# Starting the first chunk of an MLP's forward and backward pass on half its rows: eight PSUM groups on 256 rows, w1 by rows, the other rows by DMA transpose

## The chip, the cores and the metric

The kernel runs on one core of one Trainium2 chip. The metric is device time in microseconds of that core; lower is better. Besides the device time, each run lists the span of the core's own work.

## The reference

```python
def _fwd_reference(x, w1, w2):              # x: 1 x 2048 x 640, w1: 640 x 1536, w2: 1536 x 640, bf16
    h = jnp.einsum("bsd,df->bsf", x, w1)
    h = _silu(h)
    out = jnp.einsum("bsf,fd->bsd", h, w2)
    return out

def reference(x, w1, w2, grad_out):
    _out, _vjp = jax.vjp(_f, x, w1, w2)     # _f is _fwd_reference
    return (_out, *_vjp(grad_out))          # out, grad x, grad w1, grad w2
```

## The kernel before

The kernel works through 2048 rows in four chunks of 512 (`SC`). For each chunk it computes h transposed (12 groups of 128 columns of w1, each five matmuls deep, in one PSUM bank each), its SiLU and what the gradient needs, then `out` ("the second phase" below: `w2_nat` with `aT`), then the gradients. The first chunk has nothing to hide its loads behind. Its head is what the change touches:

```python
    LAG_G = 4; KM = 2; NWARM = 22
    # ... NWARM matmuls on a constant tile keep TensorE busy while x is loaded ...
    early += [load_x_half(0), load_x_half(1), load_w1_rows(0, 1), load_w1_rows(1, KM)]   # 2 x 320 KB of x, 2 x 128 KB of w1
    load_w1_rows(KM, DT)                       # columns 0:512 of the other three row blocks of w1
    for fc in range(1, NFC):
        load_w1(fc * FC, (fc + 1) * FC)        # w1 columns 512:1024, 1024:1536, 640 KB each
    nc.sync.dma_start(out=w2_nat[:], in_=w2_v[:])
    goT_next = load_goT(0)                     # DMA transpose
    # ... DMA transposes of w2 and w1 ...

    def pe_x_half(xT, half):                   # 10 TensorE transposes, 5 copies; called for both halves
        for dt_ in range(DT):
            tp = ps_h.tile([P, 2, P], dt_in, name="tp", tag="hp")
            for q in range(2):
                nc.tensor.transpose(tp[:, q, :], x_two[:, half, q, dt_ * P:(dt_ + 1) * P], ident[:])
            copy(out=xT[:, dt_, lo:lo + 2 * P].rearrange("p (s q) -> p q s", q=2), in_=tp[:])

    def h_first(xT, aT, ghT):
        # ... four banks ...
        for dt_ in range(KM):
            for ft in range(FB):               # FB = 4 groups
                h_mm(hps[ft], ft, xT, dt_, dt_ + 1)          # 512 rows of x at once
        for i in range(FT + LAG_G):            # FT = 12 groups
            if i < FT:
                # ... the rest of group i: 3 matmuls if i < FB, else 5 in a new bank ...
                silu_a(i, hps[i], aT)
            if i >= LAG_G:
                silu_grad(i - LAG_G, hps[i - LAG_G], aT, ghT)
```

## Time and profile before

| | before |
|---|---|
| device time, median of the first 3 runs | 320.69 us (320.67 to 320.93) |
| span of the profiled run | 319.4 us |
| first matmul of h | 5.30 us |
| TensorE clock reaches full rate | 6.22 us |
| second phase starts | 18.71 us |

From the page of the kernel before: the span, the busy time of each engine with its share of the span, the chain of waits by engine, and the group of all h matmuls (busy time, mean ns of one, idle time before them).

```profile
span 319.4 us, 3541 instructions
PE 314.6 (98%) x1469; PEld 146.3 (46%) x1498; DVE 102.6 (32%) x182; ACT 77.9 (24%) x142; POOL 0.7 (0%) x6
PE 98%; DMA 1%; issue 1%; DVE 0%; DVEq 0%; SPq 0%
L206 PE MATMUL hp<-xT,w_nat 128*128 128x512 bf16 x238 | 57.2, 381 | 0.1
```

TensorE is the bottleneck and almost never waits. The durations of single matmuls overlap (381 ns each, but one starts every 216 ns), so starts are what to count. Next, TensorE alone in the timeline of the first 20 us (start, duration of the stretch, engine, line, instruction, count).

```profile
0.50 2.53 PE L145 MATMUL wp<-warm 128*128 128x128 bf16 x22 [0.50 <-DVE warm L141]
3.19 2.31 PE L197 MATMUL tp<-ident,x_two 128*128 128x128 bf16 x20 [0.16 <-DMA x_two<-in_x_dram]
5.30 13.57 PE L206 MATMUL hp<-xT,w_nat 128*128 128x512 bf16 x58
18.71 1.46 PE L269 MATMUL hp<-aT,w_nat 128*128 128x512 bf16 x6
```

Here is the whole room for a better start: 22 warm-up matmuls until x arrives, 20 transposes, then h without a gap. (Two of the 60 h matmuls are missing from the records.) Last, the early transfers in the DMA view (count, KB each, median us from issue to landing). The two halves of x landed at 3.15 and 4.02 us, and w2 at 17.01 us.

```profile
w_nat<-in_w_dram SPq DMA_DIRECT2D x1, 1920.0 KB, 13.4
x_two<-in_x_dram SPq DMA_DIRECT2D x2, 320.0 KB, 3.3
w_nat<-in_w_dram SPq DMA_DIRECT2D x1, 384.0 KB, 4.5
w_nat<-in_w_dram SPq DMA_DIRECT2D x2, 128.0 KB, 3.7
```

### The profile page before, as it was taken

The page shows a single profiled execution, that of the slowest core. Times are in us where ns is not written, and L with a number is a line of the kernel's source. Part 1 is how long each engine was busy: PE and PEld are TensorE (multiplying, and loading weights), DVE is VectorE, ACT ScalarE, POOL GpSimd, SP SyncE. Part 2 cuts the span into 40 slices and gives each one's busy share as a digit, 9 for nine tenths or more (in the row PEclk, how much of TensorE's full clock was granted, in tenths as well). Part 3 has the DMA queues.
Part 4 walks back from the last instruction along what each step waited for, and adds up shares of the span by engine and source line. Part 5 has one row for each costly group of instructions (what it writes and reads, how often), then busy time and mean ns, then how long its engine had stood idle before and what let it go on. Part 6 is the DMA issues. An engine that isn't in the chain of part 4 may idle for free.

```text
span 319.4 us, 3541 instructions
## 1 busy us (share of the span) xinstructions
PE 314.6 (98%) x1469; PEld 146.3 (46%) x1498; DVE 102.6 (32%) x182; ACT 77.9 (24%) x142; POOL 0.7 (0%) x6
## 2 busy tenths in 40 slices
PE   9999999999999999999999999999999999999996
PEld 6444444444444444444444444444444444444443
DVE  3771541477410087710147741000000100001001
ACT  4960000545201254411054520110100001001100
POOL 0000000000000000000000000000000000000000
PEclk9999999999999999999999999999999999999999
DMA  8999999999999855292634079819999998995111
GB/s 282 307 180 222 246 292 264 341 263 292 293 278 271 223 190 140 86 308 76 171 114 133 2 259 267 217 30 294 265 212 257 267 240 292 253 294 182 49 37 45
DMA packets 147312, 67.33 MB, mean 211 GB/s; under 512 B 112609, under 2 KB 147041, under 8 KB 147297
## 3 DMA queue, kind: packets, MB, share of 16 engines
q1 hardware_dynamic: 147296, 67.12, 80.9%
q8 instruction: 11, 0.18, 0.2%
q14 instruction: 5, 0.03, 0.0%
HBM read 9.83 MB, written 28.97 MB: 121 GB/s over the span
## 4 chain that ended last, share of the span: by engine, by line
PE 98%; DMA 1%; issue 1%; DVE 0%; DVEq 0%; SPq 0%
PE hp L269 32%; PE hp L206 16%; PE hp L357 16%; PE hp L253 16%; PE hp L406 15%; PE hp L387 1%; DMA x_two<-in_x_dram 1%; PE tp L197 1%; DVE g L398 0%; DVEq L398 0%; SPq L434 0%
## 5 line engine op out<-in xcount | busy, mean ns | idle before, releaser
L206 PE MATMUL hp<-xT,w_nat 128*128 128x512 bf16 x238 | 57.2, 381 | 0.1
L253 PE MATMUL hp<-goT,w2T 128*128 128x512 bf16 x232 | 56.4, 379 | 0.4
L269 PE MATMUL hp<-aT,w_nat 128*128 128x512 bf16 x235 | 52.2, 379 | 0.3
L269 PE MATMUL hp<-ghT,w1T 128*128 128x512 bf16 x235 | 52.2, 379 | 0.3
L357 PE MATMUL hp<-a_blk,go_nat 128*128 128x512 bf16 x236 | 51.8, 379 | 0.2
L406 PE MATMUL hp<-gh_blk,x_nat 128*128 128x512 bf16 x219 | 48.2, 379 | 0.3
L277 ACT ACTIVATE oT<-hp 128x512 bf16<-128x512 f32 x24 | 14.3, 598 | 109.8 <-PE hp L269 109.8
L215 ACT ACTIVATE aT<-hp 128x512 bf16<-128x512 f32 x48 | 29.9, 625 | 33.0 <-PE hp L206 33.0
L206 PEld LDWEIGHTS <-w_nat 128*128 128x128 bf16 x240 | 23.6, 99 | 28.4 <-issue 0.6
L269 PEld LDWEIGHTS <-w1T 128*128 128x128 bf16 x240 | 23.5, 98 | 28.3
L357 PEld LDWEIGHTS <-go_nat 128*128 128x128 bf16 x240 | 23.5, 98 | 28.3
L253 PEld LDWEIGHTS <-w2T 128*128 128x128 bf16 x240 | 23.5, 98 | 28.3
L269 PEld LDWEIGHTS <-w_nat 128*128 128x128 bf16 x240 | 23.5, 98 | 28.4
L279 DVE CAST oT<-hp 128x512 bf16<-128x512 f32 x16 | 11.1, 692 | 77.0 <-PE hp L269 63.5
L260 DVE SCALAR_TENSOR_TENSOR ghT<-ghT,hp 128x512 bf16<-128x512 bf16 x48 | 32.5, 682 | 7.3 <-PE hp L253 7.3
L406 PEld LDWEIGHTS <-x_nat 128*128 128x128 bf16 x224 | 21.9, 98 | 26.4
L222 DVE SCALAR_TENSOR_TENSOR ghT<-aT,v 128x512 bf16<-128x512 bf16 x48 | 32.8, 687 | 0.5
L221 DVE TENSOR_SCALAR v<-t 128x512 bf16<-128x512 f32 x48 | 20.3, 426 | 30.5 <-ACT t L219 30.5
L219 ACT ACTIVATE t<-hp 128x512 f32<-128x512 f32 x48 | 29.8, 625 | 0.0
L417 DVE CAST g<-hp 128x512 bf16<-128x512 f32 x7 | 4.8, 692 | 47.0 <-PE hp L406 27.4
L367 DVE CAST g2T<-hp 128x512 bf16<-128x512 f32 x7 | 4.8, 692 | 46.1 <-PE hp L357 46.1
L365 ACT ACTIVATE g2T<-hp 128x512 bf16<-128x512 f32 x8 | 4.8, 597 | 47.0 <-PE hp L357 40.8
(20 smaller groups left out, 27.0 us busy)
## 6 DMA issues: line engine op xcount, KB each, us to landing
aT_scr<-aT SPq DMA_DIRECT2D x4, 1536.0 KB, 6.2
ghT_scr<-ghT SPq DMA_DIRECT2D x4, 1536.0 KB, 8.0
out_dram<-o_sb SPq DMA_DIRECT2D x8, 640.0 KB, 3.6
oT_scr<-oT SPq DMA_DIRECT2D x4, 640.0 KB, 3.6
go_nat<-in_grad_out_dram SPq DMA_DIRECT2D x4, 640.0 KB, 6.4
x_nat<-in_x_dram SPq DMA_DIRECT2D x4, 640.0 KB, 5.3
gxT_scr<-oT SPq DMA_DIRECT2D x4, 640.0 KB, 4.7
w_nat<-in_w_dram SPq DMA_DIRECT2D x1, 1920.0 KB, 13.4
```

The costliest lines, as they stand in the source:

```text
L206: nc.tensor.matmul(hp[:], lhsT=w1_nat[:, dt_, ft * P:(ft + 1) * P], rhs=xT[:, dt_, :], start=(dt_ == 0), stop=(dt_ == DT - 1),)
L215: nc.scalar.activation(aT[:, ft, :], hp[:], ACT.Silu)
L219: nc.scalar.activation(t[:], hp[:], ACT.Tanh, scale=0.5)
L221: nc.vector.tensor_scalar(out=v[:], in0=t[:], scalar1=-0.5, scalar2=0.5, op0=ALU.mult, op1=ALU.add)
L222: nc.vector.scalar_tensor_tensor(out=ghT[:, ft, :], in0=aT[:, ft, :], scalar=1.0, in1=v[:], op0=ALU.subtract, op1=ALU.mult)
L253: nc.tensor.matmul(gp[:], lhsT=w2T[:, dt_, ft * P:(ft + 1) * P], rhs=goT[:, dt_, :], start=(dt_ == 0), stop=(dt_ == DT - 1),)
L260: nc.vector.scalar_tensor_tensor(out=ghT[:, ft, :], in0=ghT[:, ft, :], scalar=1.0, in1=gp[:], op0=ALU.add, op1=ALU.mult)
L269: nc.tensor.matmul(op_[:], lhsT=w_all[:, ft, dt_ * P:(dt_ + 1) * P], rhs=rhs_all[:, ft, :], start=(ft == 0), stop=(ft == FT - 1),)
L277: nc.scalar.activation(oT[:, dt_, :], op_[:], ACT.Copy)
L279: nc.vector.tensor_copy(out=oT[:, dt_, :], in_=op_[:])
L357: nc.tensor.matmul(gp[:], lhsT=go_nat[:, st, dt_ * P:(dt_ + 1) * P], rhs=a_blk[:, st, :], start=(st == 0), stop=(st == ST - 1),)
L406: nc.tensor.matmul(gp[:], lhsT=x_nat[:, st, dt_ * P:(dt_ + 1) * P], rhs=gh_blk[:, st, :], start=(st == 0), stop=(st == ST - 1),)
```

## The change

Its intent is to begin h after 256 rows of x instead of 512. Eight groups fill all eight PSUM banks of the program (`ps_h` has eight buffers) on those rows, going through w1 row block by row block, so w1 is loaded in pieces of 1024 columns (2 KB rows). The other 256 rows come by a DMA transpose, which saves ten of the twenty transposes on TensorE. VectorE copies the first four banks to SBUF, so that groups 8 to 11 find banks without waiting for the gradient's tanh.

```diff
-    LAG_G = 4
-    KM = 2
-    NWARM = 22
+    NWARM = 21
+    HC = 2 * P
+    NG = 8
+    NCOPY = FT - NG
+    GC = NG * P
 ...
-        early += [load_x_half(0), load_x_half(1), load_w1_rows(0, 1), load_w1_rows(1, KM)]
-        load_w1_rows(KM, DT)
+        early += [load_x(nc.sync, 0), load_x(nc.scalar, 1)]
+        early += [load_w1(k, k + 1, slice(0, GC)) for k in range(3)]
+        load_w1(3, DT, slice(0, GC))
+        nc.sync.dma_start_transpose(out=xT_next[:, :, HC:SC], in_=x2[HC:SC, :])
+        load_w1(0, DT, slice(GC, F))
 ...
+        def pe_x(xT):                        # 10 transposes into three banks, three copies
+            slices = ((0, 1), (1, 3), (3, DT))
 ...
+            for dt_ in range(DT):
+                for ft in range(NG):
+                    h_mm(hs[ft], ft, xT, dt_, dt_ + 1, slice(0, HC))
+            for ft in range(NG):
+                h_mm(hs[ft], ft, xT, 0, DT, slice(HC, SC))
+                silu_a(ft, hs[ft], aT)
+                if ft < NCOPY:
+                    h_sb = hpool.tile([P, SC], FP32, name="h_sb")
+                    nc.vector.tensor_copy(out=h_sb[:], in_=hs[ft][:])
+                    hs[ft] = h_sb
+            for ft in range(NG, FT):
+                hs.append(ps_h.tile([P, SC], FP32, name="hp"))
+                h_mm(hs[ft], ft, xT, 0, DT)
+                silu_a(ft, hs[ft], aT)
+                silu_grad(ft - NG + NCOPY, hs[ft - NG + NCOPY], aT, ghT)
 ... (the other silu_grad follow)
```

More of the change, by code (lines that the diff above doesn't have):

```diff
@@ L137 @@
         tpool = mctx.enter_context(tc.tile_pool(name="tpool", bufs=3))
+        hpool = mctx.enter_context(tc.tile_pool(name="hpool", bufs=NCOPY))
         opool = mctx.enter_context(tc.tile_pool(name="opool", bufs=2))
@@ L165, with load_x, load_w1 @@
         xT_next = xpool.tile([P, DT, SC], dt_in, name="xT")
-        x_two = cpool.tile([P, 2, 2, D], dt_in, name="x_two")
-        def load_w1(lo, hi):
-            nc.sync.dma_start(out=w1_nat[:, :, lo:hi], in_=w1_v[:, :, lo:hi])
-        def load_x_half(half):
-            lo = half * 2 * P
-            return nc.sync.dma_start(
-                out=x_two[:, half, :, :], in_=x2[lo:lo + 2 * P, :].rearrange("(p q) d -> p q d", q=2)
-            )
-        def load_w1_rows(lo, hi):
-            return nc.sync.dma_start(out=w1_nat[:, lo:hi, 0:FC], in_=w1_v[:, lo:hi, 0:FC])
-        early += [load_x_half(0), load_x_half(1), load_w1_rows(0, 1), load_w1_rows(1, KM)]
-        load_w1_rows(KM, DT)
+        def load_x(eng, q):
+            return eng.dma_start(out=x_nat[:, q, :], in_=x_v[:, q, :])
+        def load_w1(lo, hi, cols):
+            return nc.sync.dma_start(out=w1_nat[:, lo:hi, cols], in_=w1_v[:, lo:hi, cols])
+        early += [load_x(nc.sync, 0), load_x(nc.scalar, 1)]
[3 more added lines that the diff above has]
+        load_w1(0, DT, slice(GC, F))
         start_before_entry_wait(nc, {i.ins.name for i in early})
-        for fc in range(1, NFC):
-            load_w1(fc * FC, (fc + 1) * FC)
         nc.scalar.activation(warm_a[:], warm[:, 0:1], ACT.Silu)
@@ L190, with h_mm @@
         nc.sync.dma_start_transpose(out=w1T[:], in_=w1[:, :])
-        def pe_x_half(xT, half):
-            lo = half * 2 * P
-            for dt_ in range(DT):
-                tp = ps_h.tile([P, 2, P], dt_in, name="tp", tag="hp")
-                for q in range(2):
-                    nc.tensor.transpose(tp[:, q, :], x_two[:, half, q, dt_ * P:(dt_ + 1) * P], ident[:])
-                copy = nc.scalar.copy if dt_ % 2 else nc.vector.tensor_copy
-                copy(out=xT[:, dt_, lo:lo + 2 * P].rearrange("p (s q) -> p q s", q=2), in_=tp[:])
-        pe_x_half(xT_next, 0)
-        pe_x_half(xT_next, 1)
-        def h_mm(hp, ft, xT, lo, hi):
+        def pe_x(xT):
+            slices = ((0, 1), (1, 3), (3, DT))
+            tps = [ps_h.tile([P, hi - lo, 2, P], dt_in, name="tp", tag="hp") for lo, hi in slices]
+            for q in range(2):
+                for tp, (lo, hi) in zip(tps, slices):
+                    for dt_ in range(lo, hi):
+                        nc.tensor.transpose(
+                            tp[:, dt_ - lo, q, :], x_nat[:, q, dt_ * P:(dt_ + 1) * P], ident[:]
+                        )
+            for k, (tp, (lo, hi)) in enumerate(zip(tps, slices)):
+                copy_tp = nc.scalar.copy if k % 2 else nc.vector.tensor_copy
+                copy_tp(out=xT[:, lo:hi, 0:HC], in_=tp[:].rearrange("p k q s -> p k (q s)"))
+        def h_mm(hp, ft, xT, lo, hi, cols=slice(0, SC)):
             for dt_ in range(lo, hi):
                 nc.tensor.matmul(
-                    hp[:],
+                    hp[:, cols],
                     lhsT=w1_nat[:, dt_, ft * P:(ft + 1) * P],
-                    rhs=xT[:, dt_, :],
+                    rhs=xT[:, dt_, cols],
                     start=(dt_ == 0),
@@ L232, in h_first @@
         def h_first(xT, aT, ghT):
-            hps = []
-            for ft in range(FB):
-                hps.append(ps_h.tile([P, SC], FP32, name="hp"))
-            for dt_ in range(KM):
-                for ft in range(FB):
-                    h_mm(hps[ft], ft, xT, dt_, dt_ + 1)
-            for i in range(FT + LAG_G):
-                if i < FT:
-                    if i < FB:
-                        h_mm(hps[i], i, xT, KM, DT)
-                    else:
-                        hps.append(ps_h.tile([P, SC], FP32, name="hp"))
-                        h_mm(hps[i], i, xT, 0, DT)
-                    silu_a(i, hps[i], aT)
-                if i >= LAG_G:
-                    silu_grad(i - LAG_G, hps[i - LAG_G], aT, ghT)
+            pe_x(xT)
+            hs = [ps_h.tile([P, SC], FP32, name="hp") for ft in range(NG)]
+            for dt_ in range(DT):
[13 more added lines that the diff above has]
+                silu_grad(ft - NG + NCOPY, hs[ft - NG + NCOPY], aT, ghT)
+            for ft in list(range(NCOPY)) + list(range(NG, FT)):
+                silu_grad(ft, hs[ft], aT, ghT)
         def g_group(ft, goT, ghT):
@@ L296 @@
                 for j in range(0, ST, STC):
-                    nc.sync.dma_start(out=x_nat[:, j:j + STC, :], in_=x_v[:, j:j + STC, :])
+                    rows = slice(max(j, 2), j + STC)
+                    nc.sync.dma_start(out=x_nat[:, rows, :], in_=x_v[:, rows, :])
             if c == 0:
```

## The prediction

> **What bounds the kernel.** TensorE: 98% busy of a 319.4 us span (the page), and the chain of waits is TensorE from 3.19 us to the tail. In the trace the 512-column matmuls start every 216 ns from 6.4 to 313 us without a wait. 1440 x 0.2158 = 310.8 us is fixed, and the change doesn't touch it. Only the head (first h matmul at 5.30 us) and a cold stretch (the first two h matmuls took 419 and 427 ns, full rate from about 6.2 us) can move: at most some 2 us, under 1%.
>
> **Removed.** Ten of twenty PE transposes, 107 ns apart at the cold rate: 1.07 us. The first copies wait for 320 KB of x instead of 640 KB; the two halves landed at 3.15 and 4.0 us, so x is complete near 3.1 us. Transposes run about 2.9 to 3.9 us; the copy of the first slice (0.45 us, 0.35 us after its transposes) ends near 4.2 us. First h matmul: about 4.25 us, 1.05 us earlier.
>
> **Added.** Forty more matmuls (80 of 256 columns for 40 of 512), about 2.5 ns each: 0.1 us. Weight loads stay hidden: in the last block 384-column matmuls start every 162 ns and 128-column ones every 56 ns. Four VectorE copies of about 0.69 us; VectorE (32% busy) has slack. More cold time: [...]107 ns per 128 columns before 6.2 us, 56 ns in the last block. I expect the doubling near 6.2 us again; starting 1.05 us earlier in the cold gains only half of that.
>
> **Moved.** w1 comes in 256 KB pieces. From the landings of before (320 KB at 3.15, 640 at 4.0, 1280 at 6.5 us) I estimate them at 3.9, 4.8 and 5.6 us and the 512 KB at 7.2 us. h on 256 rows needs them at 4.25, 6.0, 6.9 and 7.8 us: no wait. The DMA transpose of rows 256 to 511 follows in the queue; 640 KB transposes took 3.1 to 3.7 us of queue in the trace, so 1.6 to 1.9 us for half: landing near 9.0 us. The first eight groups reach it near 9.5 us: just no wait. w2 (landed 17.0, needed 18.7 us) comes about 0.8 us later, at 17.8; needed at 18.2: tight. goT, w2T, w1T have 7 us of slack. The first banks are free by 13 us, group 8 needs one near 13.9 us; ScalarE started activations every 0.48 us here and keeps up.
>
> **Sum.** -1.05 (earlier start) + 0.53 (cold half) + 0.1 (overhead) = -0.4 us; tight arrivals may take some back. Predicted time **320.3 us**, range 319.5 to 321.1. Chances: faster by over 2%: 0.005; within 2%: 0.985; slower by over 2%: 0.01.
>
> **What would show it.** In the timeline: first h matmul at 4.0 to 4.5 us; 213 ns per 256-column matmul until about 6.2 us, 109 ns after; the second 256 columns begin at 9.3 to 9.9 us without a TensorE gap over 0.3 us; the second phase (w2_nat with aT) starts near 18.2 us instead of 18.7; later stages unchanged. Idle TensorE before the second 256 columns would show the transpose late; idle before the second phase, w2 late.
>
> **What would make it wrong.** The transpose or w2 over 0.5 us later: no gain, or up to 1 us slower. The clock doubling earlier than 6.2 us (gain up to 1 us), or later through the gap between transposes and h. x late through the ScalarE queue. Nothing here reaches 2% (6.4 us).

(The sum: -1.05 + 0.53 + 0.1 = -0.42 us. The 0.53 us in it is an estimate from the measured 107 and 56 ns per 128 columns and from the 6.2 us of one trace.)

## The result, and the profile after

| | before | after |
|---|---|---|
| device time, median | 320.80 us (4 runs, 320.67 to 320.93) | 320.71 us (4 runs, 320.49 to 321.03) |
| span of the profiled run | 319.4 us | 319.3 us |
| first matmul of h | 5.30 us | 3.94 us |
| TensorE clock reaches full rate | 6.22 us | 3.49 us |
| second phase starts | 18.71 us | 18.57 us |

The ratio is 0.9998, with a 95% interval of 0.9981 to 1.0015. (A ratio is the mean time of one kernel's fast runs over that of the other's fast runs of the same rounds, so it isn't quite the ratio of the medians quoted here.) The two kernels can't be told apart in this test. From the page of the kernel after:

```profile
span 319.3 us, 3597 instructions
PE 313.3 (98%) x1499; PEld 148.6 (47%) x1527; DVE 103.0 (32%) x182; ACT 77.2 (24%) x139; POOL 0.7 (0%) x6
PE 96%; DMA 2%; issue 1%; DVE 0%; DVEq 0%
L204 PE MATMUL hp<-xT,w_nat 128*128 128x512 bf16 (+1 forms) x272 | 56.9, 348 | 1.8 <-DMA w_nat<-in_w_dram 1.2
```

The h matmuls now stand idle 1.8 us, mostly for w1, and the chain of waits has gained a DMA. TensorE in the timeline after:

```profile
0.50 2.42 PE L148 MATMUL wp<-warm 128*128 128x128 bf16 x21 [0.50 <-DVE warm L144]
2.71 1.10 PE L195 MATMUL tp<-ident,x_nat 128*128 128x128 bf16 x10
3.94 1.91 PE L204 MATMUL hp<-xT,w_nat 128*128 128x256 bf16 x16
6.85 1.05 PE L204 MATMUL hp<-xT,w_nat 128*128 128x256 bf16 x8 [1.00 <-DMA w_nat<-in_w_dram]
8.13 10.60 PE L204 MATMUL hp<-xT,w_nat 128*128 128x256 bf16 x75 [0.23 <-DMA w_nat<-in_w_dram]
18.57 1.67 PE L270 MATMUL hp<-aT,w_nat 128*128 128x512 bf16 x7
```

h starts 1.36 us earlier, and it runs at full rate from its first matmul (109 ns from start to start). Then it stops twice: 16 matmuls, a gap, 8 matmuls, a second gap. From start to start these gaps are 1.27 and 0.505 us where 0.109 is normal, so TensorE lost 1.16 + 0.40 = 1.56 us. The DMA view and the chain of waits (start, duration, what) name the cause. First the DMA view:

```profile
w_nat<-in_w_dram SPq DMA_DIRECT2D x1, 1920.0 KB, 13.3
w_nat<-in_w_dram SPq DMA_DIRECT2D x3, 256.0 KB, 3.8
w_nat<-in_w_dram SPq DMA_DIRECT2D x1, 512.0 KB, 6.0
x_nat<-in_x_dram SPq DMA_DIRECT2D x1, 160.0 KB, 2.6
x_nat<-in_x_dram ACTq DMA_DIRECT2D x1, 160.0 KB, 2.9
```

Then the chain of the first 20 us:

```profile
2.04 6.05 DMA w_nat<-in_w_dram
8.09 0.04 issue
8.13 6.50 PE hp L204 x57
```

The 512 KB of w1 that were issued at 2.04 us landed at 8.09 us, and everything after is TensorE without a gap. What follows that landing is fixed: 16 + 40 matmuls of 109 ns and 20 of 216 ns are 10.42 us, and 8.13 + 10.42 = 18.55 us is the start of the second phase. So in this trace the landing of the last early w1 piece sets the time, and nothing that happened before it matters.

The rest of the program did not change. The span minus the start of the second phase is 300.72 us before and 300.68 us after; over all fourteen profiles it is 300.67 to 300.72 us. The start of the second phase therefore stands for the whole kernel below.

### The profile page after: what moved, and what is told of

It reads as the page before. It is cut to its first block, busy times and chain, and to the rows that moved or that the text cites. A ratio compares the mean times of both kernels' runs of the same rounds, so it can differ in the third digit from the quotient of the medians.

```text
span 319.3 us, 3597 instructions
## 1 busy us (share of the span) xinstructions
PE 313.3 (98%) x1499; PEld 148.6 (47%) x1527; DVE 103.0 (32%) x182; ACT 77.2 (24%) x139; POOL 0.7 (0%) x6
## 4 chain that ended last, share of the span: by engine, by line
PE 96%; DMA 2%; issue 1%; DVE 0%; DVEq 0%
PE hp L270 32%; PE hp L254 16%; PE hp L359 16%; PE hp L204 15%; PE hp L408 15%; DMA w_nat<-in_w_dram 2%; PE hp L389 1%; DVE g L400 0%; DVEq L400 0%
## 5 line engine op out<-in xcount | busy, mean ns | idle before, releaser
L204 PE MATMUL hp<-xT,w_nat 128*128 128x512 bf16 (+1 forms) x272 | 56.9, 348 | 1.8 <-DMA w_nat<-in_w_dram 1.2
L204 PEld LDWEIGHTS <-w_nat 128*128 128x128 bf16 x280 | 27.1, 98 | 26.4 <-DMA w_nat<-in_w_dram 2.1
L213 ACT ACTIVATE aT<-hp 128x512 bf16<-128x512 f32 x48 | 28.6, 606 | 36.7 <-PE hp L204 36.7
L270 PEld LDWEIGHTS <-w_nat 128*128 128x128 bf16 x240 | 23.4, 98 | 28.4
L217 ACT ACTIVATE t<-hp 128x512 f32<-128x512 f32 x44 | 26.1, 598 | 0.5 <-DVE v L219 0.5
```

The lines of the kernel that those rows point to most:

```text
L204: nc.tensor.matmul(hp[:, cols], lhsT=w1_nat[:, dt_, ft * P:(ft + 1) * P], rhs=xT[:, dt_, cols], start=(dt_ == 0), stop=(dt_ == DT - 1),)
L213: nc.scalar.activation(aT[:, ft, :], hp[:], ACT.Silu)
L217: nc.scalar.activation(t[:], hp[:], ACT.Tanh, scale=0.5)
L270: nc.tensor.matmul(op_[:], lhsT=w_all[:, ft, dt_ * P:(dt_ + 1) * P], rhs=rhs_all[:, ft, :], start=(ft == 0), stop=(ft == FT - 1),)
```

## The experiments

All twelve runs gave correct results. Two readings need a word. "Full rate at" is the time at which the clock records of a trace show the TensorE clock going from half to full; three traces (b_nogap, a_gap, a_xone) have no such record, and there it is read from the spacing of the matmuls. "w1 complete" is the landing of the last piece of w1 that the first 256 rows need in the changed kernel; it is taken from the last of the sixteen counts of that transfer's semaphore in the trace (which DMA engine a count is from, the trace does not say). The record lists chip 6 for the four runs of experiment 1, chip 2 for a_swap, a_1kb, v1 and v2, chip 4 for a_xtwo and v3, and chip 9 for a_xone and v4. Times are compared with the kernel before in the same job; landings compared between jobs are one trace each, on different chips. The edits are shown shortened, with helpers written out in place.

| profile | full rate at | first h | w1 complete | second phase | span |
|---|---|---|---|---|---|
| before | 6.22 | 5.30 | - | 18.71 | 319.43 |
| b_rep | 6.16 | 5.25 | - | 18.66 | 319.36 |
| b_nogap | 4.0 | 5.40 | - | 18.36 | 319.07 |
| after | 3.49 | 3.94 | 8.09 | 18.57 | 319.26 |
| a_rep | 5.44 | 3.94 | 8.02 | 18.51 | 319.19 |
| a_gap | 8.2 | 4.35 | 7.90 | 19.30 | 319.98 |
| a_swap | 3.22 | 3.85 | 7.78 | 19.41 | 320.09 |
| a_1kb | 6.52 | 3.94 | 8.14 | 18.44 | 319.13 |
| a_xtwo | 5.22 | 4.42 | 7.30 | 23.08 | 323.78 |
| a_xone | 3.8 | 4.34 | 7.55 | 18.04 | 318.74 |
| v1 | 3.63 | 3.98 | - | 18.44 | 319.11 |
| v2 | 4.35 | 3.95 | - | 19.56 | 320.24 |
| v3 | 5.28 | 3.94 | - | 17.99 | 318.69 |
| v4 | 3.87 | 4.02 | - | 17.54 | 318.21 |

### 1. The same two kernels again, and the warm-up made longer or shorter

The first traces left two questions. Did the clock come early in the kernel after because its TensorE had no gap (the kernel before has one of 0.4 us before its transposes), or by chance, from run to run? And does the clock matter at all, if w1 sets the pace?

```diff
# a_rep: the kernel after, unaltered.   b_rep: the kernel before, unaltered.
# b_nogap, in the kernel before:
-    NWARM = 22
+    NWARM = 26
# a_gap, in the kernel after:
-    NWARM = 21
+    NWARM = 17
```

> The changed kernel again, unaltered, to see what repeats. If its early doubling of the TensorE clock (3.5 us in the first trace, against 6.2 us in the kernel before) comes from the unbroken TensorE activity, it is again within 0.3 us of 3.5 us[...]. If the late w1 pieces (third piece at 6.8 us, last at 8.1 us) come from the pieces themselves, TensorE waits again 1.5 to 2.1 us for w1 before the second 256 columns; if they were a chance lag of some DMA engines, the wait is under 0.8 us or very different. Time 320.5 to 321.0.

> The kernel before, unaltered, against itself: the noise floor, ratio 1.000 within 0.001. The gap theory says that the clock doubles again at 6.2 us within 0.3[...]. First h matmul at 5.3 us.

> The kernel before with 26 warm-up matmuls instead of 22, which closes its idle TensorE gap of 0.4 us before the transposes. Gap theory: the clock doubles near 3.5 us, the transposes run at 56 ns from there, the first h matmul starts at 4.7 to 5.1 us (the second half of x lands at 4.0 us), nothing is cold after it, and the time falls by 0.5 to 1.0 us to about 320.0. Chance theory: doubling time and kernel time as in the kernel before, within 0.2 us.

> The changed kernel with 17 warm-up matmuls instead of 21, which opens a gap of about 0.4 us before its transposes, as the kernel before has one. Gap theory: the clock doubles at 5.5 to 6.9 us, h on 256 rows runs at 213 ns until then, yet because w1 was late anyway, the end of h comes only 0 to 0.5 us later. Chance theory: no systematic change of the doubling time. If w1 sets the pace, time within 0.4 us of the changed kernel in either case.

Measured, all four beside the same 11 runs of the kernel before (median 321.55 us, median span 319.0): a_rep 320.96 us, ratio 0.9981 (0.9964 to 0.9998); b_rep 321.08 us, 0.9991 (0.9972 to 1.0009); b_nogap 320.99 us, 0.9986 (0.9971 to 1.0001); a_gap 320.92 us, 0.9989 (0.9970 to 1.0009). The interval of the kernel against itself (b_rep) overlaps the other three, so these times separate nothing. The median spans say the same: 319.0 for the kernel before, 319.2 for the kernel after.

The profiles say more. The kernel after, unaltered, reached full rate at 3.49 us in one trace and at 5.44 us in the other, with hardly a gap in either. So the gap theory in its simple form has fallen. (b_rep came to full rate at 6.16 us, as the gap theory had said, but by chance it could have too.) TensorE in the repeated run (timeline):

```profile
3.94 1.75 PE L204 MATMUL hp<-xT,w_nat 128*128 128x256 bf16 x8
6.11 12.56 PE L204 MATMUL hp<-xT,w_nat 128*128 128x256 bf16 x91 [0.42 <-DMA w_nat<-in_w_dram]
18.51 1.67 PE L270 MATMUL hp<-aT,w_nat 128*128 128x512 bf16 x7
```

Its first eight h matmuls ran at the half clock, 213 ns apart, yet the second phase began 0.06 us earlier than in the first trace: the waits for w1 shrank (0.51 and 0.20 us, from 0.723 us between starts where 0.213 was normal, and from 0.306 where 0.109 was) and the last early piece landed at nearly the same time. The smaller waits do not mean that w1 was earlier: the second piece landed at 6.07 us, the third at 6.69 and the last at 8.02, but the slow matmuls asked for them later. In both traces the second phase began 10.49 us after the last landing (8.09 and 8.02 us). In this kernel an earlier clock buys nothing until w1 arrives earlier.

The reverse case is a_gap. Its edit did not open the gap where it was meant to: x had landed early enough for the transposes to follow the warm-up at once, at 2.34 us. The gap, 0.97 us, came before the first h matmul, whose w1 piece landed at 4.30 us:

```profile
4.35 15.12 PE L204 MATMUL hp<-xT,w_nat 128*128 128x256 bf16 x99 [0.76 <-DMA w_nat<-in_w_dram]
```

Full rate came only at 8.2 us, the matmuls were 213 ns apart until then, and no wait for w1 was left after the first. The second phase began at 19.30 us, 0.8 us later than in a_rep and outside its expectation; 10.49 us after its last early piece (7.90 us) would have been 18.39 us. So the clock matters once it is later than w1. (This is one profile: the median spans of the six runs each, 319.15 us for a_gap and 319.2 for a_rep, don't differ.)

What sets the moment of full rate is not shown. Over all fourteen traces it came 2.7 to 6.0 us after the first warm-up matmul (at 3.22 to 6.52 us, the first at 0.5 us), and 7.7 us after it in a_gap, where 0.97 us of idle time came between. In the ten traces whose clock records show one stretch at full rate, it lasted 314.03 us (as in the kernel before) or 317.44 us (as in the kernel after). The gap of the kernel before, between 2.82 and 3.19 us, is not shown to be the reason for its late clock: a_rep, with hardly a gap, came to full rate only 0.8 us earlier. Nor does b_nogap test it, though it had full rate at 4.0 us: two traces of the unaltered kernel after lie 1.95 us apart.

In one run the clock also fell back: a_xtwo of experiment 3, where TensorE stood still from 5.5 to 9.4 us. Its clock records go to full rate at 5.22 us, back to half at 8.64 us, 3.1 us after TensorE had stopped, and to full again at 12.05 us, 2.6 us after it had started again (3.42 and 3.41 us from one change to the next). In the table of stretches (span, length, then for each engine busy time and number of instructions; the last three columns are the TensorE clock, the DMA share and GB/s) the clock column follows:

```profile
5.00:6.00 1.00, 0.61 (x5) 0.34 (x3) 0.00 (x0) 0.00 (x0) 0.00 (x0) 1.00 0.92 330
10.00:11.00 1.00, 1.00 (x7) 0.73 (x5) 0.00 (x0) 0.00 (x0) 0.00 (x0) 0.50 1.08 362
13.00:14.00 1.00, 1.00 (x12) 0.90 (x10) 0.00 (x0) 0.00 (x0) 0.00 (x0) 1.00 1.08 367
```

### 2. What makes w1 late: the transpose behind it, or its row size?

The prediction had put the last early w1 piece at 7.2 us; it landed at 8.09, 8.02 and 7.90 us. Two suspects were tried.

```diff
# a_swap: the transpose of x one place back in the queue
         load_w1(3, DT, slice(0, GC))
-        nc.sync.dma_start_transpose(out=xT_next[:, :, HC:SC], in_=x2[HC:SC, :])
         load_w1(0, DT, slice(GC, F))
+        nc.sync.dma_start_transpose(out=xT_next[:, :, HC:SC], in_=x2[HC:SC, :])
# a_1kb: the same bytes of w1 in 1 KB rows, matmuls in the order of the pieces
-        early += [load_w1(k, k + 1, slice(0, GC)) for k in range(3)]
-        load_w1(3, DT, slice(0, GC))
+        early += [load_w1(0, 2, slice(lo, lo + FC)) for lo in (0, FC)]
+        early += [load_w1(2, DT, slice(0, FC))]
+        load_w1(2, DT, slice(FC, GC))
```

> The changed kernel with the DMA transpose of rows 256 to 511 moved one place back in the queue, behind the last third of w1. If the transpose behind it is what holds up the landing of the last early w1 piece (7.9 to 8.1 us in three traces), that piece lands by 7.4 us and the DMA rate in the seventh microsecond no longer falls to 104 to 133 GB/s. If the piece is late by its own (2 KB rows, uneven engines), it lands at 7.7 to 8.2 us as before. In either case the transposed x lands near 11 us, TensorE waits over 1.5 us for it before the second 256 columns, and the second phase starts 1 to 2 us later than 18.5 us.

> The changed kernel with the same w1 bytes in as many early transfers (256, 256, 384, 384 KB), but in 1 KB row pieces instead of 2 KB ones, and the order of the 256-column matmuls changed to match. If 2 KB rows are what makes w1 late, the rate between 3 and 7 us rises from 283 to 297 GB/s to 320 or more and the last of the four pieces lands by 7.4 us; the second phase then starts near 18.0 us. If not the row size but the amount of w1 (1280 KB for 256 rows of x) and the transpose behind it, it lands again at 7.8 to 8.2 us and the second phase starts at 18.4 to 18.7 us.

Measured: a_swap 321.96 us, ratio 1.0028 (1.0009 to 1.0048); a_1kb 320.81 us, 0.9990 (0.9967 to 1.0012). Without the transpose behind it the piece landed at 7.78 us, inside what the second theory had allowed; with 1 KB rows it landed at 8.14 us. By these single traces neither is the main cause; up to 0.3 us may be the transpose's. a_swap also shows what the place of a transfer in the queue costs: x landed at 10.69 us instead of 9.38, TensorE waited for it, and the second phase moved to 19.41 us.

In these traces the transpose did cost something, for those around it. The rate fell to 123 GB/s for a microsecond in the kernel after, and the dip moved with the transpose: in a_swap the same microsecond had 376 GB/s, and the next two 233 and 206. The stretch from 7 to 8 us is first that of the kernel after, then that of a_swap, followed by a_swap's next two (the last column is GB/s):

```profile
7.00:8.00 1.00, 0.90 (x8) 0.56 (x6) 0.00 (x0) 0.00 (x0) 0.00 (x0) 1.00 0.72 123
```

```profile
7.00:8.00 1.00, 0.67 (x7) 0.36 (x5) 0.00 (x0) 0.00 (x0) 0.00 (x0) 1.00 1.07 376
8.00:9.00 1.00, 1.00 (x11) 0.90 (x10) 0.00 (x0) 0.00 (x0) 0.00 (x0) 1.00 1.56 233
9.00:10.00 1.00, 0.75 (x7) 0.52 (x6) 0.00 (x0) 0.00 (x0) 0.00 (x0) 1.00 0.94 206
```

Another thing in the traces was not in the prediction's reckoning: the sixteen counts of one transfer don't come together. In the kernel after, the first count of the third w1 piece came at 4.74 us, the fifteenth at 6.67 and the last at 6.81. TensorE waited for the last: its next matmul started at 6.85 us. In the kernel before, the same spread was 7.08 to 9.91 us for its fourth w1 transfer, which was only just in time. In the trace of the kernel after, the first and the last count were 0.7 to 2.1 us apart for the 256 KB pieces of w1; in that of the kernel before, up to 2.9 us for a 640 KB piece. A landing time estimated from the mean rate is an estimate for the average count.

One more thing shows in the counts. With the transpose behind it, the last early piece was counted nearly all at once (from 7.94 to 8.09 us in the kernel after, and within 0.15 us in a_gap, a_1kb and a_xone too); without it, in a_swap, from 6.34 to 7.78 us. So the middle count came 1.4 us later with the transpose behind it (8.03 against 6.64 us, the eighth of sixteen), and the last one's 0.3 us. The data were late too, and not only the counts: the last 2 KB packet of w1 ended at 7.74 us in the kernel after and at 7.37 us in a_swap.

### 3. The form of the load of x

The traces of the kernel after moved 266 to 308 GB/s between 3 and 6 us, those of the kernel before 311 to 351 (bytes of the packets that ended in each microsecond, mean of three; three traces of each, b_nogap and a_gap among them). The two ranges almost touch. The load of x differs: two transfers of 1280 B rows on two queues instead of 2560 B rows on one.

```diff
# a_xtwo: one transfer, two neighbouring rows per partition (and NWARM = 24)
-        early += [load_x(nc.sync, 0), load_x(nc.scalar, 1)]
+        early += [nc.sync.dma_start(out=x_nat[:, 0:2, :], in_=x2[0:HC, :].rearrange("(p q) d -> p q d", q=2))]
 ...
-                copy_tp(out=xT[:, lo:hi, 0:HC], in_=tp[:].rearrange("p k q s -> p k (q s)"))
+                copy_tp(out=xT[:, lo:hi, 0:HC].rearrange("p k (s q) -> p k q s", q=2), in_=tp[:])
# a_xone: one transfer, 1280 B rows (and NWARM = 24)
-        early += [load_x(nc.sync, 0), load_x(nc.scalar, 1)]
+        early += [nc.sync.dma_start(out=x_nat[:, 0:2, :], in_=x_v[:, 0:2, :])]
```

> The changed kernel, but its first 256 rows of x come as in the kernel before: one transfer, two neighbouring rows (2560 B) to a partition, on one queue, instead of two of 1280 B rows on two queues; 24 warm-up matmuls bridge to its landing near 3.0 us. If the form of the x load or the second queue is what lowers the DMA rate of the changed kernel between 3 and 6 us (266 to 308 GB/s in its traces[...]), the rate is 320 or more, the last early w1 piece lands by 7.5 us and the second phase starts near 18.0 us. If not, it lands at 7.8 to 8.2 us and the second phase starts at 18.4 to 18.7 us.

> The changed kernel with its first 256 rows of x in one transfer on one queue, still in 1280 B rows; 24 warm-up matmuls. In the run with 2560 B rows on one queue the last early w1 piece landed at 7.31 us and the rate from 3 to 6 us was 333 GB/s, but copies there waited for the DMA transpose by a dependence that the edit had made, so its time says nothing. If one queue was the reason, this run has a rate of 320 or more, w1 complete by 7.5 us, and the second phase at 17.8 to 18.2 us; if the 2560 B rows were, or chance, the rate is 266 to 308, w1 is complete at 7.8 to 8.2 us and the second phase starts at 18.4 to 18.7 us.

Measured: a_xtwo 326.79 us, ratio 1.0175 (1.0152 to 1.0198). This run is a lesson in reading, not in x loads. Its strided copy gave the program a dependence on the DMA transpose into the same tile (they touch different columns), and TensorE stood for 3.8 us. One line of its waits shows it:

```profile
PE hp L204 <- ACT xT L200: 3.8, 1, 3.8
```

Its transfers were still as intended: w1 complete at 7.30 us, with 333 GB/s between 3 and 6 us. a_xone, which has no such dependence, had w1 complete at 7.55 us, with 304 GB/s, and its second phase began at 18.04 us, 0.5 us earlier than in the traces of the kernel after and again 10.49 us after the landing. But its time was 320.76 us, ratio 0.9991 (0.9976 to 1.0006), and its median span 319.0 against 319.1 for the kernel before. By its expectation the rate spoke for chance or row size, the second phase for one queue, while the landing fell between the two ranges given. In one profile each, x in one transfer on one queue brought w1 some 0.4 to 0.8 us earlier; that it does so reliably is not shown, and whether rows, queue or only another chip did it stays open. In these traces the second queue gained nothing in rate: 266 to 308 GB/s with two queues, 333 and 304 with one.

### 4. Less w1 before the rows of x: versions meant to beat both

If the amount of w1 is what holds up the changed kernel, the cure is to need less of it. In the changed kernel each 256 KB of w1 feeds eight matmuls of 109 ns, 0.87 us of work at full rate: an estimate from these numbers is that TensorE asks for 300 GB/s of w1 (262,144 bytes in 0.872 us), about as much as was delivered at this point (266 to 308 GB/s between 3 and 6 us). v1 keeps the early start on 256 rows but goes back to four groups; its first 256 rows need 640 KB of w1 instead of 1280. v2 is v1 with all of x transposed on TensorE. v3 then splits the two pieces that v1 was seen to wait for, and v4 splits w2.

```diff
# v1, against the kernel after (no bank copies; LAG_G = 4 as in the kernel before)
-        early += [load_w1(k, k + 1, slice(0, GC)) for k in range(3)]
-        load_w1(3, DT, slice(0, GC))
+        early += [load_w1(0, 2, slice(0, FC)), load_w1(2, DT, slice(0, FC))]
         nc.sync.dma_start_transpose(out=xT_next[:, :, HC:SC], in_=x2[HC:SC, :])
-        load_w1(0, DT, slice(GC, F))
+        for lo in range(FC, F, FC):
+            load_w1(0, DT, slice(lo, lo + FC))
 ...
-                for ft in range(NG):
+                for ft in range(FB):
                     h_mm(hs[ft], ft, xT, dt_, dt_ + 1, slice(0, HC))
 ... (then 256 columns for groups 0 to 3, and groups 4 to 11 on 512)
# v2, against v1: rows 256:512 loaded plainly between the two w1 pieces, 10 transposes after the first 8 matmuls
-        nc.sync.dma_start_transpose(out=xT_next[:, :, HC:SC], in_=x2[HC:SC, :])
+        early += [nc.sync.dma_start(out=x_nat[:, 2:4, :], in_=x_v[:, 2:4, :])]
# v3, against v1
-        early += [load_w1(0, 2, slice(0, FC)), load_w1(2, DT, slice(0, FC))]
+        early += [load_w1(0, 2, slice(0, FC)), load_w1(2, 3, slice(0, FC)), load_w1(3, DT, slice(0, FC))]
-        for lo in range(FC, F, FC):
-            load_w1(0, DT, slice(lo, lo + FC))
+        load_w1(0, 2, slice(FC, 2 * FC))
+        load_w1(2, DT, slice(FC, 2 * FC))
+        load_w1(0, DT, slice(2 * FC, F))
+                if i == FB:                      # groups 4 to 7 piece by piece, in four banks
+                    hs += [ps_h.tile([P, SC], FP32, name="hp") for ft in range(FB)]
+                    for dt_ in range(2):
+                        for ft in range(FB, 2 * FB):
+                            h_mm(hs[ft], ft, xT, dt_, dt_ + 1)
# v4, against v3
-        nc.sync.dma_start(out=w2_nat[:], in_=w2_v[:])
+        for lo in (0, FT // 2):
+            nc.sync.dma_start(out=w2_nat[:, lo:lo + FT // 2, :], in_=w2_v[:, lo:lo + FT // 2, :])
```

> A version meant to beat both: the start of the changed kernel (256 rows of x first, three-bank transposes), but four groups on 512 columns of w1 as in the kernel before, so that the first 256 rows need 640 KB of w1 instead of 1280 KB; rows 256 to 511 by DMA transpose right behind these 640 KB; no VectorE copies. If the amount of w1 sets the pace of the changed kernel, the four groups wait under 0.5 us for w1, the transposed x lands at 6.5 to 7.3 us, and the second phase starts at 17.3 to 18.1 us: 0.5 to 1.2 us faster than both, span near 318.0. If the DMA transpose's own delay sets it, x lands after 7.5 us and the gain is under 0.4 us.

> As v1, but rows 256 to 511 come by a plain load between the two w1 pieces and are transposed on TensorE after the first eight matmuls: no DMA transpose before the second phase. Amount theory: second phase at 17.6 to 18.3 us, a little later than v1 for the ten transposes (0.56 us warm). If DMA transposes hold up the queue, v2 is better than v1.

> v1 with the two waits it showed taken on: its second w1 piece (384 KB, landed at 5.5 us, 0.76 us wait) split into 128 and 256 KB, and the w1 for groups 4 to 7 (640 KB, landed at 9.76 us, 1.1 us wait) split into 256 and 384 KB, with these four groups run piece by piece in four banks. Theory: TensorE waits for the bytes of the piece it needs next. Then the waits fall from 1.9 us in all to under 0.8 us and the second phase starts at 17.3 to 17.9 us, span 318.0 to 318.6. Rival: the slowest DMA engine is late for whatever is queued, so a split piece lands no earlier than the whole: the second phase stays at 18.2 to 18.6 us.

> v3 with w2 in two transfers of six row blocks each. In v3 the only wait left in the head was 0.41 us before the second phase, for w2, which landed whole at 17.94 us with a DMA transpose behind it. If the wait is for the completion of the one large transfer, the first half lands by 15 us, the second before its use 1.3 us into the phase, and the second phase starts with the last h matmul, 17.3 to 17.7 us: 0.2 to 0.5 us faster than v3, ratio to the kernel before 0.996 to 0.997. If the landing is late because the DMA transpose behind holds all engines, the wait only moves to the seventh matmul of the second phase, and the time equals v3's.

| run | time, us | beside it, before | ratio (95%) | median span, before |
|---|---|---|---|---|
| v1 | 320.87 | 321.12 | 0.9993 (0.9972 to 1.0014) | 319.1, 319.2 |
| v2 | 321.75 | 321.12 | 1.0018 (1.0002 to 1.0034) | 319.9, 319.2 |
| v3 | 320.33 | 321.04 | 0.9975 (0.9962 to 0.9989) | 318.5, 319.3 |
| v4 | 320.06 | 320.91 | 0.9971 (0.9958 to 0.9983) | 318.3, 319.1 |

v1 missed its expectation. x landed at 6.73 us as hoped, and the waits had moved to the next pieces: 384 KB of w1 landed at 5.50 us, needed at 4.89, and the 640 KB for groups 4 to 7 at 9.75 us, needed at 9.05 (its last count was 0.7 us behind the fifteenth). From start to start TensorE lost 0.65 and 0.75 us. (The expectation of v3 puts these waits at 0.76 and 1.1 us, which is more than the starts show.)

```profile
5.54 3.67 PE L201 MATMUL hp<-xT,w_nat 128*128 128x256 bf16 x32 [0.49 <-DMA w_nat<-in_w_dram]
9.79 8.81 PE L201 MATMUL hp<-xT,w_nat 128*128 128x512 bf16 x39 [0.58 <-DMA w_nat<-in_w_dram]
```

v2 was worse: its x landed at 5.82 us, 1.6 us after its first count, its second w1 piece at 7.38 us, and TensorE waited twice. A large amount less at the very start is not enough when the next transfers are just as tight.

v3 took on exactly these two waits by splitting the pieces, with the same bytes in the same order. They then landed at 4.29 and 5.13, and at 8.41 and 9.44 us, and h ran from its first matmul to its last without a wait for w1 over 0.2 us. The rival, that a split piece lands no earlier than the whole, fell for the first parts, by one trace each. The second phase, at 17.99 us, still missed the expected 17.3 to 17.9. v3 is the first version that is faster than the kernel before with an interval clear of 1, by 0.25%. Its only large wait left was for w2 (17.94 us), which v4 took away: its first half landed at 13.49 us and its second at 17.33, before its first use, 1.3 us into the phase. TensorE in v3, then in v4:

```profile
3.94 13.80 PE L202 MATMUL hp<-xT,w_nat 128*128 128x256 bf16 x79
17.99 3.19 PE L271 MATMUL hp<-aT,w_nat 128*128 128x512 bf16 x14 [0.24 <-ACT aT L211]
```

```profile
4.02 2.50 PE L203 MATMUL hp<-xT,w_nat 128*128 128x256 bf16 x20
6.72 10.98 PE L203 MATMUL hp<-xT,w_nat 128*128 128x256 bf16 x60 [0.20 <-DMA xT<-in_x_dram]
17.54 3.83 PE L272 MATMUL hp<-aT,w_nat 128*128 128x512 bf16 x17
```

The bracket in v3's second line names ScalarE, but that is only 0.24 us before the matmuls; the weight load of the same line waited 0.7 us for w2 in the list of waits, and v4, which changed only the loading of w2, has no wait there. In v4 the second phase follows the last h matmul at once, at 17.54 us: 1.17 us earlier than in the trace of the kernel before (18.71). Of that, the runs hold 0.8 us in the median spans (318.3 against 319.1) and 0.3% in time. v3 and v4 ran in different jobs, so the step between them is shown by the profile, not by the times.

## Why the prediction was right or wrong

The time, 320.3 us with a range of 319.5 to 321.1, held 320.71 us, and "within 2%" held too. Point by point:

- **The bound, and that only the head can move: right.** What follows the start of the second phase took 300.67 to 300.72 us in all fourteen profiles. The added matmuls and weight loads were hidden (109 ns per 256 columns), and VectorE and ScalarE were never waited for in a way that counts.
- **First h matmul near 4.25 us: right, a little pessimistic.** It was 3.94 us in both traces of the changed kernel.
- **"I expect the doubling near 6.2 us again": wrong.** It came at 3.49 us in the first trace and 5.44 us in the second; over all profiles it was between 3.2 and 8.2 us. I had read one trace's value as a property of the kernel. The rule that I used for the time to the doubling is not shown by any trace here: in the trace of the kernel before, the doubling came 5.7 us after the first warm-up matmul. What that trace shows is the two rates, 107 and 56 ns per 128 columns.
- **"h on 256 rows needs them at 4.25, 6.0, 6.9 and 7.8 us: no wait": wrong, and this is the step that failed.** The pieces landed at 3.89, 4.75, 6.81 and 8.09 us, against estimates of 3.9, 4.8, 5.6 and 7.2. The first two were right to 0.05 us in this trace (in a_rep the second came at 6.07). The third and fourth came 1.2 and 0.9 us late. I had applied the mean rate of the kernel before (351 GB/s between 3 and 6 us in its trace, against 266 here), and I had counted for the average of the sixteen counts, while TensorE waited for the last one (6.81 us for the third piece, whose first came at 4.74; the next matmul at 6.85). Why the rate was lower is not shown. The same step also took its deadlines from the late clock: with full rate from the start they were 3.94, 4.8, 5.7 and 6.6 us (an estimate from 109 ns a matmul). Together this made 1.56 us of waits where none were foreseen.
- **"the second 256 columns begin at 9.3 to 9.9 us without a TensorE gap over 0.3 us": right.** x landed at 9.38 us (9.0 predicted), and its first matmul came at 9.9 us after the eighth group, without a gap. w2, called tight, landed at 18.10 us, 0.47 us before it was needed.
- **The sum, -0.4 us: the earlier start is right, the sum is three times too large, and the total time fits partly by luck.** The second phase began at 18.57 us instead of the predicted 18.2, which is 0.14 us earlier than before. Against the prediction, the start was 0.30 us better, the cold half of 0.98 us after 4.25 us was not paid at all, and 1.56 us of waits came in: 18.2 - 0.30 - 0.98 + 1.56 = 18.48 us. In the repeated run the start was again 0.30 us better, 0.75 us of cold loss was paid, and 0.71 us of waits: 18.2 - 0.30 - 0.23 + 0.71 = 18.38 us, measured 18.51. Two errors of opposite sign made a good total, which is luck. They are not independent: a late clock hides late data, and early data would have uncovered a late clock.

So the change did what it meant to do, an h that starts 1.36 us earlier, and gave it back as waits for w1. Its eight groups on 256 rows ask for twice the w1 per unit of TensorE work than four groups on 512 rows do, while the queue moved 266 to 308 GB/s and 300 were asked for. In the three traces of this form with an early enough clock (after, a_rep, a_xone) the second phase began 10.49 us after the last early piece of w1, whether that landed at 8.09 or at 7.55 us. That a version with the same start and smaller, well placed pieces gains 0.8 us of span (v4) supports this; that the amount of w1 alone was not the whole matter is shown by v1, which halved it and gained nothing.

What stays open: why single 2 KB packets of w1 took up to 1.6 us around 4 us, where 84 ns was usual, and why the counts of one transfer come so far apart; what sets the moment at which the clock doubles; and whether one transfer of x on one queue reliably brings w1 forward (a_xone's times do not show it).

## What to carry to other kernels

At a cold start, list for each early transfer when its last count lands (in these traces up to 2.9 us after its first) and when its first use is due, at full clock; the largest of the delays is the loss, and starting earlier than the data only moves it. Reusing a weight over fewer rows raises the weight bytes needed per microsecond of matmul (here to 300 GB/s on 256 rows, the estimate of experiment 4), so shrink both operands of the first piece together, and cut the pieces along the order in which they are used. Don't take the moment at which the TensorE clock doubles from one trace: it moved by five microseconds among these kernels (3.2 to 8.2 us), and by two between two runs of one of them (3.49 and 5.44 us).
